# Score tiles of both heads in one double bank, and partition maxima by way of memory, in a fused attention and feed-forward kernel

## The chip, the cores and the metric

The kernel runs on one core of one Trainium2 chip. The metric is the device time of one execution in microseconds. The kernel before took 1224.53 us (median of three runs, 1223.8 to 1225.92). TensorE is called PE here (its weight loads PEld), VectorE DVE, ScalarE ACT, GpSimd POOL, and SyncE, which issues every DMA of this kernel, SP.

## The reference

Attention with a decay for 8 batches of 8 heads, 576 positions and 64 channels, and then a feed-forward layer with a quadratic gate over the 4608 tokens:

```python
log_f = np.log(np.clip(f, 0.0001, 1.0))
cum = np.cumsum(log_f, axis=-1)
scores = scale * q @ k.T + (cum[:, :, :, None] - cum[:, :, None, :])   # causal, scale = 1/8
attn = softmax(scores); attn_out = attn @ v
h = attn_out.reshape(4608, 512) @ w_in                                  # 512 -> 2048
g = np.where(h >= 1, h, np.where(h <= -1, 0.0, (h + 1) ** 2 / 4))
out = g @ w_out                                                         # 2048 -> 512
```

## The kernel before

The kernel works in f16 pairs: a number is scaled by a power of two and split into a high and a low f16 part, and a product takes three matmuls. The scale needs the largest magnitude of a tensor over all 128 partitions, which is what `across` (L112) gives: it takes one or two columns of maxima per partition, transposes them on PE (L120), reduces and clamps the row on DVE (L122, L123), spreads it over a diagonal (L127), broadcasts that to all partitions by a matmul with ones (L130) and copies the result (L131). It is called 48 times: for the 16 weight blocks (`weight_split`), for v of each of the 8 batches (`value_scale`), and for q and k together of 24 jobs (`measure`).

A job is a pair of heads of one batch. Batch 0 is cut into two row ranges, so there are 36 jobs. In the first 12, scores are made from f32 operands (`early_prepare`), and in the first 5 the probabilities are turned by PE (`turn_rows`); in that time the 16 weight blocks are loaded and split too. The other 24 jobs use split f16 operands and turn probabilities by DMA transposes (`pT`).

`scores` makes one block of 128 query rows: for each term and each of the two heads one matmul over 64 partitions, head 0 on partitions 0 to 63 and head 1 on 64 to 127 (L470). The outputs lie in tiles of the ring `s`, one bank for each head and two banks in all. The last block has 64 rows and 576 columns; both heads lie in the partitions of one tile of two banks, `big`, of which there is one. `big` also takes the values (`values`, `early_values`), the transposes of `early_prepare` and those of the decay sums. `weights` reads the scores on DVE (L559, with the decay row that POOL prepared from `ck` at L476 and L480), takes the exponential on ACT (L563), and splits the scaled probabilities into `pr` (L577 on ACT, L583 on DVE).

The feed-forward layer is cut into 144 units of 256 tokens and 256 hidden channels: `moe_front` (L645) into the ring `ph` of two banks, `moe_back` (L673) into `po0` and `po1`. Units are put between the rows of later jobs as tokens become ready; those left over run alone at the end.

v is loaded a second time for its maximum, by four loads per batch at L245 and reductions at L246. From batch 1 on these loads use the ring `ck` of three buffers, which also holds the decay rows that `load_decay` brings (L343).

The code gives the order in which work is recorded. The order on each engine and queue is made at build time by a scheduler with a model of the chip: it takes an instruction when its inputs, and a free buffer, are there by its model. Each engine then runs its list in order, and SP issues DMAs in order, each with its waits.

Of the kernel before, what the change touches and what calls it, by code (L numbers as in the profile page):

```python
# [8 lines left out]
F32 = mybir.dt.float32  # L9
# [37 lines left out]
def kernel(  # L47
# [41 lines left out]
    tiny = ctx.enter_context(tc.tile_pool(name="tiny", bufs=4))  # L89
    dram = ctx.enter_context(tc.tile_pool(name="dram", bufs=1, space=bass.MemoryType.DRAM))  # L90
    ps = ctx.enter_context(tc.tile_pool(name="ps", bufs=2, space=bass.MemoryType.PSUM))
    ps1 = ctx.enter_context(tc.tile_pool(name="ps1", bufs=1, space=bass.MemoryType.PSUM))
# [19 lines left out]
    def across(dst, m):  # L112

        n = m.shape[1]
        pt = ps.tile([P, 512], F32, name="s")
        nc.tensor.transpose(pt[0:n, 0:P], m, ident)  # L120
        top = tiny.tile([P, 1], F32, name="top", bufs=2)
        nc.vector.tensor_reduce(out=top[0:n], in_=pt[0:n, 0:P], axis=AX.X, op=ALU.max)  # L122
        nc.vector.tensor_scalar(  # L123
            out=top[0:n], in0=top[0:n], scalar1=LOW, scalar2=HIGH, op0=ALU.max, op1=ALU.min
        )
        dg = tiny.tile([P, 2], F32, name="dg", bufs=2)
        nc.vector.tensor_scalar(  # L127
            out=dg[0:n, 0:n], in0=ident[0:n, 0:n], scalar1=top[0:n], scalar2=None, op0=ALU.mult
        )
        nc.tensor.matmul(pt[:, P:P + n], lhsT=ones[0:n], rhs=dg[0:n, 0:n], start=True, stop=True)  # L130
        nc.vector.tensor_copy(dst, pt[:, P:P + n])  # L131


    ident = const.tile([P, P], F32, name="ident")
    make_identity(nc, ident)
    ones = const.tile([2, P], F32, name="ones")
    nc.gpsimd.memset(ones, 1.0)
    cum_d = dram.tile([B * H, S], F32, name="cum_d")
    cq = const.tile([P, NT5, B * H], F32, name="cq")

    def decay_sums():
# [93 lines left out]
    bsc = {}  # L235

    def value_scale(b):
        m4 = tiny.tile([P, NPAIR], F32, name="m4", bufs=2)
        for i in range(NPAIR):
            if b:  # L240
                st = two.tile([P, S], F32, name="ck", bufs=3)
            else:
                st = stage[:, i * S:(i + 1) * S]
            part = v[b, 2 * i:2 * i + 2].rearrange("h s d -> (h s d)").rearrange("(p n) -> p n", p=P)
            nc.sync.dma_start(st, part)  # L245
            nc.vector.tensor_reduce(  # L246
                out=m4[:, i:i + 1], in_=st, axis=AX.X, op=ALU.max, apply_absolute_value=True
            )
        m1 = tiny.tile([P, 1], F32, name="m1", bufs=2)
        nc.vector.tensor_reduce(out=m1, in_=m4, axis=AX.X, op=ALU.max)  # L250
        m = mv[:, b:b + 1]
        across(m, m1)
        if b:
            nc.vector.tensor_tensor(out=m, in0=m, in1=mv[:, b - 1:b], op=ALU.max)
        scale_of(sv[:, b:b + 1], pv[:, b:b + 1], m)
# [100 lines left out]
    def early_prepare(w):  # L356

        if w.p == 0:
            nc.vector.tensor_scalar(out=cq8, in0=cq[:, :, 0:2 * H], scalar1=8.0, scalar2=None, op0=ALU.mult)
        t_ = early_qk[(w.p + NQK) % 2]  # L360
        w.nsig, w.nalpha = -8.0, -0.125
        bh = w.b * H + 2 * w.hp
        w.cqs = cq8[:, :, bh:bh + 2]
        w.terms = ((t_[:, 0], t_[:, 1]),)
        for j in range(2):
            pt = ps1.tile([P, 1024], F32, name="big")
            t0 = 0 if j else w.r0
            n = w.s1 - P * t0
            for c0 in range(0, n, P):
                m = min(P, n - c0)  # L370
                nc.tensor.transpose(pt[:, c0:c0 + m], w.x32[j][0:m, c0:c0 + P], ident[0:m, 0:m])
            nc.scalar.activation(t_[:, j, 0:n], pt[:, 0:n], AF.Copy)
# [75 lines left out]
    def scores(w, r):  # L448
# [4 lines left out]
        for h in range(2):  # L453
            at.append((0, P) if r < LAST else (64 * h, 64 * h + 64))
            if r < LAST or h == 0:
                if r < LAST:
                    ring = sdr + more if w.p < NPE else sdr
                    sp = ps.tile([P, 512], F32, name="s")
                else:
                    ring = sd4 + [prs[LAST]] if w.p < NPE else sd4  # L460
                    sp = ps1.tile([P, 1024], F32, name="big")
                sd = ring[turn[r < LAST] % len(ring)]
# [56 lines left out]
    def early_values(w, x):  # L519
        if w.r0 == 0 and len(w.cuts) == 1:  # L520
            av = [ps1.tile([P, DM], F32, name="po0")]
        else:
            big = ps1.tile([P, 1024], F32, name="big")
            av = [big[:, 0:512], big[:, 512:1024]]
# [71 lines left out]
    def values(w, x):  # L596
        av = ps1.tile([P, 1024], F32, name="big")
        at = 512 - w.cuts[0][1] if len(w.cuts) == 2 else -w.s0
# [142 lines left out]
    load_decay(pairs[0], 1)  # L741
    prepare(pairs[0])
    value_scale(0)
    split_values(pairs[0])
    for p in range(njobs + 1):
# [3 lines left out]
        if w:  # L749
# [9 lines left out]
            def step(r):  # L759
                if r + 1 < w.r1:  # L760
                    scores(w, r + 1)
                if r == w.r1 - 2 and nxt:
                    load_decay(nxt, 1)
                    if nxt.hp == 0 and nxt.r0 == 0:
                        value_scale(nxt.b)
                    split_values(nxt)
                weights(w, r)
                if r == w.r1 - 1 and p + 2 < njobs:
                    measure(pairs[p + 2])
# [62 lines left out]
```

## Time and profile before

| | |
|---|---|
| median of three runs | 1224.53 us |
| profiled execution, its own time | 1223.2 us |
| its span, first to last instruction | 1221.4 us |
| mean granted TensorE clock | 0.954 |
| DMA moved | 152.21 MB in 408541 packets |

In the profile, a row of a group gives line, engine, operation, tiles, count, then busy time and mean length, then the idle time before these instructions and what ended it. The timeline gives start, length, engine, line, tiles and count. In the waits, a row names who waited, for whom, how long in total, how often, and the longest. PE's ends are modelled and matmuls overlap, so the steps between starts tell what a matmul costs PE's stream.

### The profile page before, as it was taken

Reading aid. Unit: us, or ns where it says so; the run is one execution under the profiler, and the core shown is the slowest. Engines: PE = TensorE matmul, PEld = TensorE weight load, DVE = VectorE, ACT = ScalarE, POOL = GpSimd, SP = SyncE. Lnnn points to the kernel's source line nnn. Section 1 sums busy time; section 2 is a strip of 40 time slices with the busy share of each in tenths; the row PEclk is TensorE's granted clock in tenths of the full one; section 3 lists DMA queues with packets and bytes.
Section 4 is the critical chain, followed back from the end, with each engine's and each line's share of the span. In section 5 each row is a group of like instructions: output and inputs, shape, how many; then the busy total and the mean of one; then the engine's idle time right before and its main releaser. Section 6 shows DMA issues by size and latency. Waiting matters only on the chain.

```text
span 1221.4 us, 24896 instructions
## 1 busy us (share of the span) xinstructions
PE 1118.6 (92%) x8865; PEld 683.2 (56%) x8865; DVE 854.6 (70%) x2423; ACT 762.5 (62%) x1558; POOL 443.9 (36%) x695
## 2 busy tenths in 40 slices
PE   5587677996799999999999999989999999999998
PEld 3354334553456565565655665655665566567665
DVE  6889888776877787777666767777877796522222
ACT  3574665774756676757666667666767687644443
POOL 4758644542633254334333224432443263100000
PEclk9878788899699999999999999999999999999999
DMA  8957543768866768657636736666966685300000
GB/s 230 278 149 199 135 123 79 138 126 175 172 129 140 146 131 162 126 120 141 126 88 134 150 69 126 140 138 123 172 123 135 143 154 114 72 24 2 18 19 18
DMA packets 408541, 152.21 MB, mean 125 GB/s; under 512 B 384225, under 2 KB 385249, under 8 KB 408417
## 3 DMA queue, kind: packets, MB, share of 16 engines
q1 hardware_dynamic: 408416, 150.63, 57.7%
q8 instruction: 69, 1.13, 0.4%
q14 instruction: 56, 0.45, 0.1%
HBM read 75.64 MB, written 9.58 MB: 70 GB/s over the span
## 4 chain that ended last, share of the span: by engine, by line
PE 38%; DVE 5%; DMA 3%; issue 2%; SPq 2%; ACT 2%; POOL 0%; DVEq 0%; ACTq 0%
PE ph L645 16%; PE po L673 16%; PE s L470 3%; PE big L603 2%; DMA ck<-in_v_dram 1%; DVE pr L583 1%; DVE sdr L559 1%; SPq L332 1%; DMA qk<-in_k_dram 1%; PE big L470 1%; DMA qk<-in_q_dram 1%; DVE u L656 1%; DVE g L659 1%; SPq L429 0%; ACT pr L577 0%
## 5 line engine op out<-in xcount | busy, mean ns | idle before, releaser
L645 PE MATMUL ph<-x,place 128*128 128x256 f16 (+3 forms) x4608 | 449.9, 250 | 12.6 <-DVE u L656 7.9
L673 PE MATMUL po<-place,g 128*128 128x512 f16 x1728 | 423.7, 384 | 9.4 <-DVE g L659 5.8
L645 PEld LDWEIGHTS <-place 128*128 128x128 f16 x4608 | 356.0, 99 | 115.2 <-issue 44.8
L673 PEld LDWEIGHTS <-g 128*128 128x128 f16 x1728 | 161.3, 99 | 184.8 <-issue 21.1
L476 POOL TENSOR_SCALAR sdr<-ck,nsig,cqs 128x128 f32<-128x128 f32 (+1 forms) x192 | 155.9, 815 | 229.8 <-DVE pr L583 218.1
L563 ACT ACTIVATE sdr<-sdr,nm 128x384 f32<-128x384 f32 (+1 forms) x248 | 138.5, 559 | 95.1 <-DVE nm L559 84.8
L470 PE MATMUL s<-qkT 64*128 64x384 f16 (+6 forms) x704 | 158.9, 359 | 23.3 <-DVE nm L559 21.6
L656 DVE SCALAR_TENSOR_TENSOR u<-ph,z,u 128x512 f32<-128x512 f32 x136 | 101.6, 747 | 108.8 <-ACT u L655 108.2
L654 ACT ACTIVATE u<-ph,z 128x512 f32<-128x512 f32 x136 | 104.7, 769 | 111.3 <-PE ph L645 110.6
L658 ACT ACTIVATE g<-u,z 128x512 f16<-128x512 f32 x136 | 97.7, 718 | 90.8 <-DVE u L656 90.2
L577 ACT ACTIVATE pr<-sdr,rc 128x384 f16<-128x384 f32 (+1 forms) x236 | 120.0, 556 | 38.7 <-DVE rc L574 16.9
L583 DVE SCALAR_TENSOR_TENSOR pr<-sdr,rc,pr 128x384 f16<-128x384 f32 (+2 forms) x232 | 126.3, 573 | 25.4 <-ACT pr L577 24.2
L476 POOL TENSOR_SCALAR sd<-ck,nsig,cqs 64x576 f32<-64x576 f32 x48 | 54.2, 1130 | 242.6 <-ACT qs L403 91.0
L659 DVE SCALAR_TENSOR_TENSOR g<-u,z,g 128x512 f16<-128x512 f32 x136 | 103.6, 761 | 38.4 <-ACT g L658 38.2
L559 DVE CUSTOM_DVE_ANT_0 sdr<-s,sdr,nalpha 128x128 f32<-128x128 f32 (+1 forms) x192 | 103.2, 545 | 23.1 <-PE s L470 17.0
L470 PEld LDWEIGHTS <-qkT 64*128 64x128 f16 (+1 forms) x864 | 47.9, 99 | 88.0 <-issue 66.5
L480 POOL TENSOR_SCALAR_AFFINE_SELECT sdr<-sdr 128x128 f32<-128x128 f32 x248 | 92.2, 381 | 10.9
L655 ACT ACTIVATE u<-u 128x512 f32<-128x512 f32 x144 | 89.8, 623 | 2.5
L603 PE MATMUL big<-pT,vs 128*64 128x320 f16 (+3 forms) x1098 | 72.8, 284 | 0.9 <-DVE nm L559 0.5
L381 DVE TENSOR_REDUCE m2q<-qk 128x1 f32<-128x640 f32 x48 | 39.2, 817 | 44.2 <-DMA qk<-in_q_dram 34.6
L603 PEld LDWEIGHTS <-vs 128*64 128x64 f16 x1098 | 49.9, 112 | 28.8 <-issue 10.1
L476 POOL TENSOR_SCALAR sdr<-ck,cq 128x384 f32<-128x384 f32 (+3 forms) x56 | 41.1, 734 | 62.5 <-DVE pr L583 34.1
(161 smaller groups left out, 1092.7 us busy)
## 6 DMA issues: line engine op xcount, KB each, us to landing
ck<-cum_d SPq DMA_DIRECT2D x64, 288.0 KB, 3.6
out_dram<-ot SPq DMA_DIRECT2D x36, 256.0 KB, 2.6
qk<-in_k_dram SPq DMA_DIRECT2D x64, 128.0 KB, 2.9
ck<-in_v_dram SPq DMA_DIRECT2D x28, 288.0 KB, 2.9
v<-in_v_dram SPq DMA_DIRECT2D x62, 128.0 KB, 2.8
qk<-in_q_dram SPq DMA_DIRECT2D x56, 128.0 KB, 2.7
place<-in_moe_w_in_dram SPq DMA_DIRECT2D x12, 512.0 KB, 5.4
place<-in_moe_w_out_dram SPq DMA_DIRECT2D x10, 512.0 KB, 6.7
```

What stands on the lines that cost most here:

```text
L470: nc.tensor.matmul(sds[h % len(sds)][1][p0:p1, c0:c1], lhsT=a[rows, q0 - w.s0:q0 - w.s0 + p1 - p0], rhs=b[rows, c0:c1], start=(i == 0), st ...
L476: nc.gpsimd.tensor_scalar(out=sd[p0:p1, 0:wid], in0=w.ck[h][p0:p1, 0:wid], scalar1=w.nsig if w.p < NQK else w.nsig[p0:p1], scalar2=w.cqs[p ...
L559: nc.vector.tensor_tensor_reduce(out=a, in0=sp[:, 0:wid], in1=a, scale=w.nalpha, scalar=BIG, op0=ALU.add, op1=ALU.min, accum_out=nm[:, i:i ...
L563: nc.scalar.activation(a, a, AF.Exp, bias=nm[:, i:i + 1], scale=-1.0, accum_out=sm[:, i:i + 1])
L577: nc.scalar.activation(pr[:, :, 0, i, :], a, AF.Copy, scale=rc[:, i:i + 1])
L583: nc.vector.scalar_tensor_tensor(out=pr[:, :, 1, i, :], in0=a, scalar=rc[:, i:i + 1], in1=pr[:, :, 0, i, :], op0=ALU.mult, op1=ALU.subtract,)
L603: nc.tensor.matmul(av[64 * h:64 * h + 64, at + s0:at + s1], lhsT=w.vs[:, vl, h, t, :], rhs=w.pT[:, t, pl, h, s0:s1], start=(t == 0 and pi ...
L645: nc.tensor.matmul(ph[:, fi, a0:a1], lhsT=wi[fb][:, wl, t, fi * P:(fi + 1) * P], rhs=xs[b][:, t, xl, s0:s0 + a1 - a0], start=(fi == 0 and ...
L654: nc.scalar.activation(u, h, AF.Relu, scale=z.u[:, i:i + 1], bias=z.h[:, i:i + 1])
L656: nc.vector.scalar_tensor_tensor(out=u, in0=h, scalar=z.t[:, i:i + 1], in1=u, op0=ALU.max, op1=ALU.min)
L659: nc.vector.scalar_tensor_tensor(out=g[:, 1], in0=u, scalar=z.r[:, i:i + 1], in1=g[:, 0], op0=ALU.mult, op1=ALU.subtract)
L673: nc.tensor.matmul(po[ch][i], lhsT=g[:, gl, fi * TC + i * P:fi * TC + (i + 1) * P], rhs=wo[fb][:, wl, fi, :], start=(first and fi == 0 and ...
```

## The change

It has three parts. The two heads' scores of a row block share one tile of two banks, one bank for each head; the ring `s` has two such tiles, and everything that used `big` now uses it, so PSUM has the same eight banks in use. `across` writes the columns of maxima to a row in memory, loads this row into all partitions, and reduces it on DVE; PE has no part in it. And v's loads for its maximum have a ring of their own, `vst`, and are recorded in the row blocks of the third pair of the batch before, with the maximum itself in the first row block of the fourth pair.

```diff
+    dram2 = ctx.enter_context(tc.tile_pool(name="dram2", bufs=4, space=bass.MemoryType.DRAM))
...
     def across(dst, m):
         n = m.shape[1]
-        pt = ps.tile([P, 512], F32, name="s")
-        nc.tensor.transpose(pt[0:n, 0:P], m, ident)
-        top = tiny.tile([P, 1], F32, name="top", bufs=2)
-        nc.vector.tensor_reduce(out=top[0:n], in_=pt[0:n, 0:P], axis=AX.X, op=ALU.max)
-        nc.vector.tensor_scalar(
-            out=top[0:n], in0=top[0:n], scalar1=LOW, scalar2=HIGH, op0=ALU.max, op1=ALU.min
-        )
-        dg = tiny.tile([P, 2], F32, name="dg", bufs=2)
-        nc.vector.tensor_scalar(
-            out=dg[0:n, 0:n], in0=ident[0:n, 0:n], scalar1=top[0:n], scalar2=None, op0=ALU.mult
-        )
-        nc.tensor.matmul(pt[:, P:P + n], lhsT=ones[0:n], rhs=dg[0:n, 0:n], start=True, stop=True)
-        nc.vector.tensor_copy(dst, pt[:, P:P + n])
+        d = dram2.tile([1, P * n], F32, name=f"row{n}")
+        nc.sync.dma_start(d.rearrange("o (p n) -> (o p) n", n=n), m)
+        rows = two.tile([P, 2 * P], F32, name="rows")[:, 0:n * P]
+        nc.sync.dma_start(rows, d.broadcast_to([P, n * P]))
+        nc.vector.tensor_reduce(
+            out=dst, in_=rows.rearrange("a (p n) -> a n p", n=n), axis=AX.X, op=ALU.max
+        )
+        nc.vector.tensor_scalar(out=dst, in0=dst, scalar1=LOW, scalar2=HIGH, op0=ALU.max, op1=ALU.min)
...
+    def value_part(b, i):
+        if b not in vmax:
+            vmax[b] = tiny.tile([P, NPAIR], F32, name="m4", bufs=2)
+        if b:
+            st = two.tile([P, S], F32, name="vst")
+        else:
+            st = stage[:, i * S:(i + 1) * S]
...
     def value_scale(b):
-        m4 = tiny.tile([P, NPAIR], F32, name="m4", bufs=2)
-        for i in range(NPAIR):
-            if b:
-                st = two.tile([P, S], F32, name="ck", bufs=3)
...
-            pt = ps1.tile([P, 1024], F32, name="big")
+            pt = ps.tile([P, 1024], F32, name="s")
...
                     ring = sdr + more if w.p < NPE else sdr
-                    sp = ps.tile([P, 512], F32, name="s")
                 else:
                     ring = sd4 + [prs[LAST]] if w.p < NPE else sd4
-                    sp = ps1.tile([P, 1024], F32, name="big")
+                if h == 0:
+                    pair = ps.tile([P, 1024], F32, name="s")
+                sp = pair[:, 512 * h:512 * h + 512] if r < LAST else pair
...
     def values(w, x):
-        av = ps1.tile([P, 1024], F32, name="big")
+        av = ps.tile([P, 1024], F32, name="s")
...
                 if r == w.r1 - 2 and nxt:
                     load_decay(nxt, 1)
-                    if nxt.hp == 0 and nxt.r0 == 0:
-                        value_scale(nxt.b)
                     split_values(nxt)
                 weights(w, r)
+                if w.r1 == NT5 and w.b + 1 < B:
+                    i = r - w.r0
+                    if w.hp == NPAIR - 2:
+                        for part in range(i, i + 1 if r < LAST else max(i, NPAIR)):
+                            if part < NPAIR:
+                                value_part(w.b + 1, part)
+                    if w.hp == NPAIR - 1 and i == 0:
+                        value_scale(w.b + 1)
```

The order on PE in the fourteenth job (its operands are `qkT_3210` before and `qkT_3115` after), at the third row block, 384 columns wide; `s_3597` is head 0 and `s_3598` head 1. Before:

```order
L470 LDWEIGHTS qkT_3210
L470 MATMUL s_3597<-qkT_3210 128x384
L645 LDWEIGHTS place0_90
L645 MATMUL ph_3646<-x_80,place0_90 128x192
...
L645 MATMUL ph_3646<-x_80,place0_90 128x192
L470 LDWEIGHTS qkT_3210
L470 MATMUL s_3598<-qkT_3210 128x384
```

The same row block after, where both heads lie in `s_3493` and L466 and L641 are the lines of scores and feed-forward:

```order
L466 MATMUL s_3493<-qkT_3115 128x384
L466 LDWEIGHTS qkT_3115
L466 MATMUL s_3493<-qkT_3115 128x384
L641 LDWEIGHTS place0_90
L641 MATMUL ph_3541<-x_81,place0_90 128x64
```

Before, 19 feed-forward matmuls stood between the three matmuls of one head and the three of the other. After, the six stand in one run, the heads taking turns.

On DVE, a maximum of q and k (tile `m2q_7190`, reduced at L376) and its return from memory (L120), in a job of the second half. After:

```order
L376 TENSOR_REDUCE m2q_7190<-qk32_0_114 128x1
L579 SCALAR_TENSOR_TENSOR pr1_5960<-sdr_2_119,rc_5967,pr1_5960 128x2x128
L579 SCALAR_TENSOR_TENSOR pr1_5960<-sdr_3_120,rc_5967,pr1_5960 128x2x128
L567 TENSOR_SCALAR rc_6068<-sm2_6063 128x2
L570 RECIPROCAL rc_6068<-rc_6068 128x2
L652 SCALAR_TENSOR_TENSOR u_6027<-ph_5978,z_5435,u_6027 128x512
L579 SCALAR_TENSOR_TENSOR pr2_6061<-sdr_0_117,rc_6068,pr2_6061 128x3x128
L579 SCALAR_TENSOR_TENSOR pr2_6061<-sdr_1_118,rc_6068,pr2_6061 128x3x128
L120 TENSOR_REDUCE mk_7193<-rows_7196 128x2
L555 ISA sdr_2_119,nm_6177<-s_6046,sdr_2_119,nalpha_5296 128x512
```

Seven instructions stand between the reduction and the one that reads the row; the score minimum behind it (L555, which was L559) waits with it. On SP the same maximum stands between this job's k loads and the decay rows, `qkT` of the next job and `pT` of the current one:

```order
L327 DMA qk32_0_114<-in_k_dram 128x4x64 x2
L331 DMA qk32_0_114<-in_k_dram 64x2x64
L117 DMA row2_7194<-m2q_7190 128x2
L119 DMA rows_7196<-row2_7194 128x256
L338 DMA ck_6168<-cum_d_88 128x576
L338 DMA ck_6409<-cum_d_88 128x576
L405 DMA_TRANSPOSE qkT_6416<-qs_6411 128x20x128
L585 DMA_TRANSPOSE pT_5925<-pr0_5926 128x4x128
```

Before, SP went from the k loads to the decay rows with no store and no load of a row between them.

More of the change, by code (lines that the diff above doesn't have):

```diff
@@ L118, in across @@
         n = m.shape[1]
-        pt = ps.tile([P, 512], F32, name="s")
-        nc.tensor.transpose(pt[0:n, 0:P], m, ident)
-        top = tiny.tile([P, 1], F32, name="top", bufs=2)
-        nc.vector.tensor_reduce(out=top[0:n], in_=pt[0:n, 0:P], axis=AX.X, op=ALU.max)
-        nc.vector.tensor_scalar(
-            out=top[0:n], in0=top[0:n], scalar1=LOW, scalar2=HIGH, op0=ALU.max, op1=ALU.min
-        )
-        dg = tiny.tile([P, 2], F32, name="dg", bufs=2)
-        nc.vector.tensor_scalar(
-            out=dg[0:n, 0:n], in0=ident[0:n, 0:n], scalar1=top[0:n], scalar2=None, op0=ALU.mult
-        )
-        nc.tensor.matmul(pt[:, P:P + n], lhsT=ones[0:n], rhs=dg[0:n, 0:n], start=True, stop=True)
-        nc.vector.tensor_copy(dst, pt[:, P:P + n])
+        d = dram2.tile([1, P * n], F32, name=f"row{n}")
[4 more added lines that the diff above has]
+            out=dst, in_=rows.rearrange("a (p n) -> a n p", n=n), axis=AX.X, op=ALU.max
+        )
+        nc.vector.tensor_scalar(out=dst, in0=dst, scalar1=LOW, scalar2=HIGH, op0=ALU.max, op1=ALU.min)
     ident = const.tile([P, P], F32, name="ident")
     make_identity(nc, ident)
-    ones = const.tile([2, P], F32, name="ones")
-    nc.gpsimd.memset(ones, 1.0)
     cum_d = dram.tile([B * H, S], F32, name="cum_d")
@@ L235 @@
     bsc = {}
-    def value_scale(b):
-        m4 = tiny.tile([P, NPAIR], F32, name="m4", bufs=2)
-        for i in range(NPAIR):
-            if b:
-                st = two.tile([P, S], F32, name="ck", bufs=3)
[L242 to L247, printed above, removed]
-            )
+    vmax = {}
+    def value_part(b, i):
[5 more added lines that the diff above has]
+            st = stage[:, i * S:(i + 1) * S]
+        part = v[b, 2 * i:2 * i + 2].rearrange("h s d -> (h s d)").rearrange("(p n) -> p n", p=P)
+        nc.sync.dma_start(st, part)
+        nc.vector.tensor_reduce(
+            out=vmax[b][:, i:i + 1], in_=st, axis=AX.X, op=ALU.max, apply_absolute_value=True
+        )
+    def value_scale(b):
         m1 = tiny.tile([P, 1], F32, name="m1", bufs=2)
-        nc.vector.tensor_reduce(out=m1, in_=m4, axis=AX.X, op=ALU.max)
+        nc.vector.tensor_reduce(out=m1, in_=vmax[b], axis=AX.X, op=ALU.max)
         m = mv[:, b:b + 1]
@@ L365, in early_prepare @@
         for j in range(2):
-            pt = ps1.tile([P, 1024], F32, name="big")
+            pt = ps.tile([P, 1024], F32, name="s")
             t0 = 0 if j else w.r0
@@ L522, in early_values @@
         else:
-            big = ps1.tile([P, 1024], F32, name="big")
+            big = ps.tile([P, 1024], F32, name="s")
             av = [big[:, 0:512], big[:, 512:1024]]
@@ L742 @@
     prepare(pairs[0])
+    for i in range(NPAIR):
+        value_part(0, i)
     value_scale(0)
```

## The prediction

> **What bounds the kernel now.** I read the page's busy times first, then the windows of three stages, then the waits and the groups by line inside the middle stage. On the page:
>
> ```profile
> span 1221.4 us, 24896 instructions
> PE 1118.6 (92%) x8865; PEld 683.2 (56%) x8865; DVE 854.6 (70%) x2423; ACT 762.5 (62%) x1558; POOL 443.9 (36%) x695
> ```
>
> The windows of the first twelve jobs (scores in f32, weights converted), of the other 24 (scores in f16), and of the tail with feed-forward units alone:
>
> ```profile
> core 0: us, PE busy (x) PEld busy (x) DVE busy (x) ACT busy (x) POOL busy (x), PEclk, DMA share, GB/s
> 0.00:286.00 286.00, 221.66 (x1247) 125.35 (x1248) 228.31 (x704) 173.63 (x391) 154.96 (x223) 0.86 0.66 164
> 286.00:1052.00 766.00, 731.76 (x6261) 445.16 (x6258) 576.51 (x1651) 517.07 (x1064) 288.93 (x472) 0.98 0.66 133
> 1052.00:1222.00 170.00, 165.13 (x1364) 112.65 (x1360) 49.76 (x70) 71.80 (x104) 0.00 (x0) 1.00 0.10 23
> ```
>
> The middle stage holds 63% of the span. PE is busy 732 of its 766 us (96%), DVE 75%, ACT 68%: there the time is PE's stream, and PE idles 34 us. In the first stage no engine is full; in the tail PE is, with work that the change leaves alone. So the change is worth what it takes out of PE's stream between 286 and 1052 us, less what the other queues then cannot follow.
>
> **Scores.** PE's timeline (start, length, engine, line, tiles, count):
>
> ```profile
> 617.30 0.66 PE L470 MATMUL s<-qkT 64*128 64x384 f16 x3
> 617.89 0.40 PE L645 MATMUL ph<-x,place 128*128 128x64 f16 x4
> ...
> 622.04 0.82 PE L470 MATMUL s<-qkT 64*128 64x512 f16 x3
> 622.79 0.83 PE L645 MATMUL ph<-x,place 128*128 128x256 f16 x6
> 623.55 0.82 PE L470 MATMUL s<-qkT 64*128 64x512 f16 x3
> 624.31 0.28 PE L645 MATMUL ph<-x,place 128*128 128x256 f16 x1
> ```
>
> ```profile
> 428.43 0.67 PE L470 MATMUL s<-qkT 64*128 64x384 f16 x6
> 429.03 1.04 PE L673 MATMUL po<-place,g 128*128 128x512 f16 x4
> ```
>
> ```profile
> 626.48 1.69 PE L645 MATMUL ph<-x,place 128*128 128x256 f16 x14
> ```
>
> Starts count, since ends are modelled. The run of 14 gives (1.69 - 0.27) / 13 = 0.109 us for 256 columns, 0.42 ns a column. Three matmuls of 512 columns should then take 0.65 us, but the next line starts 0.75 us later; six of 256 should take 0.65 and take 0.76. So every step between a matmul on half the rows and one on all rows costs 0.105 us, and **a visit to the scores costs 0.21 us** beside its columns. And six 384-column matmuls, three of each head, took 0.60 us (428.43 to 429.03), as long as three of one head alone (617.30 to 617.89): heads on partitions 0-63 and 64-127 run side by side, **the second head is free**, if nothing stands between them.
>
> Counted over PE's order, the f16 scores of 128-row blocks are 576 matmuls and 184,320 columns in both kernels. Before, they stand in 161 visits, 24 of which hold both heads, with 18,688 columns beside the other head; after, in 100 visits, 97 with both heads, with 89,856. Before: 161 x 0.21 + 165,632 x 0.42 ns = 103 us. After: 100 x 0.21 + 94,464 x 0.42 ns = 61 us. **Minus 42 us.** The last block (64 rows) already ran its heads side by side.
>
> **Maxima off PE.** A maximum in the middle stage:
>
> ```profile
> 604.12 0.27 PE L120 MATMUL s<-ident,m2q 128*2 128x128 f32 x1
> 604.23 2.73 PE L645 MATMUL ph<-x,place 128*128 128x192 f16 x46
> 606.89 0.38 PE L130 MATMUL s<-dg,ones 2*128 2x2 f32 x2
> 607.20 0.29 PE L645 MATMUL ph<-x,place 128*128 128x192 f16 x2
> ```
>
> The transpose holds the stream 0.11 us, the broadcast 0.31 and a step of 0.1 ahead of it: 0.52 us. The groups inside the window 286 to 1052:
>
> ```profile
> L130 PE MATMUL s<-dg,ones 2*128 2x2 f32 (+1 forms) x58 | 10.4, 258 | 3.0 <-DVE dg L127 2.9
> ...
> L120 PE MATMUL s<-ident,m 128*1 128x128 f32 x6 | 1.6, 272 | 1.9 <-DVE m L250 1.9
> ```
>
> 58 broadcasts are 29 maxima, with two lost or outside records some 31: **minus 16 us**, the 5 us of waits in these rows not counted. PE's order of values and last blocks has some 20 more changes of tile shape after than before: **plus 2 us**.
>
> DVE gives up four small instructions for two:
>
> ```profile
> L122 DVE TENSOR_REDUCE top<-s 1x1 f32<-1x128 f32 (+1 forms) x48 | 12.6, 272 | 4.2 <-PE s L120 4.0
> ...
> L246 DVE TENSOR_REDUCE m<-ck 128x1 f32<-128x576 f32 x28 | 21.0, 752 | 26.2 <-DMA ck<-in_v_dram 26.0
> ```
>
> The new reduction reads 128 or 256 numbers per partition: between 0.27 and 0.75 us by these rows, I take 0.4, since 256 lies nearer to 128. With the clamp it replaces one of the same kind, so DVE loses some 0.2 us each; nothing waits for that.
>
> **The trip through memory.** No row shows it. The nearest are the store of the sums and the loads of 128 KB:
>
> ```profile
> cum_d<-x SPq DMA_DIRECT2D x1, 144.0 KB, 2.3
> ...
> qk<-in_k_dram SPq DMA_DIRECT2D x42, 128.0 KB, 2.7
> place<-in_moe_w_out_dram SPq DMA_DIRECT2D x10, 512.0 KB, 6.7
> ```
>
> The trip lies between 2 x 2.3 and 2 x 6.7 us; I take 2.3 + 2.7 = 5.0, since 128 KB is the size of the load for two columns. The way over PE was no shorter where queues were full: for the first weight block DVE's rows stand 16 us apart.
>
> ```profile
> 27.19 0.14 DVE L216 TENSOR_REDUCE m<-ms 128x1 f32<-128x2 f32 x1
> ...
> 43.41 0.16 DVE L131 COPY mi<-s 128x1 f32<-128x1 f32 x1 [1.10 <-PE s L130]
> ```
>
> What counts is how much stands on DVE between the maximum and its return. The groups give the durations:
>
> ```profile
> L583 DVE SCALAR_TENSOR_TENSOR pr<-sdr,rc,pr 128x384 f16<-128x384 f32 (+2 forms) x232 | 126.3, 573 | 25.4 <-ACT pr L577 24.2
> ...
> L656 DVE SCALAR_TENSOR_TENSOR u<-ph,z,u 128x512 f32<-128x512 f32 x136 | 101.6, 747 | 108.8 <-ACT u L655 108.2
> ...
> L381 DVE TENSOR_REDUCE m2q<-qk 128x1 f32<-128x640 f32 x48 | 39.2, 817 | 44.2 <-DMA qk<-in_q_dram 34.6
> ```
>
> In the piece of the order shown with the change, four L583, one L656 and two small ones stand between: 4 x 0.57 + 0.75 + 0.35 = 3.4 us. Added up so over the whole order, 18 of the 24 maxima of q and k have about 3.5 us; those of the weights have 3 to 31, mostly over 5. Where it is 3.5, DVE stands 5.0 - 3.5 = 1.5 us at least, and those behind it are a score minimum, on which the next scores wait. 18 x 1.5 = 27 us of DVE; PE has a feed-forward unit in hand that covers part. Bounds: nothing, and 24 x 5.0 = 120 us. I take **plus 20 us**, near the 27.
>
> The Trainium skill ("DMA: Bandwidth & Descriptors", Anatomy of one DMA) gives a fixed cost of about 2.0 us per DMA, most of it the receipt of the write, and calls HBM the heaviest target, which speaks against two small DMAs in a row. By it alone the trip would be 4.0 us and the term about 9; the 2.3 us of this trace's store agree, its loads are slower.
>
> **Waits that go.** In the middle stage and, below, in the first:
>
> ```profile
> PE s L470 <- DVE nm L559: 13.3, 8, 6.1
> ...
> POOL sd L476 <- DMA ck<-cum_d: 73.4, 22, 13.3
> ```
>
> ```profile
> PE s L120 <- DVE m L216: 14.8, 3, 10.4
> ...
> PE s L130 <- DVE dg L127: 11.4, 6, 3.0
> ```
>
> Values and the last block now share the ring of two double banks, so a row's scores can still wait for DVE: I leave the 13.3 us where they are. Own buffers for v free the decay rows' ring; POOL's 73.4 us are off the path, so I count nothing. In the first stage PE's 26 us behind maxima go, but there DVE and ACT set the pace, and the order puts the weights' ends later among the jobs; f32 heads side by side help a little. I take **minus 4 us**, bounds minus 25 and plus 20.
>
> **Sum.** -42 - 16 + 2 + 20 - 4 = -40 us. Against the profiled execution's own 1223.2 us that is 1183; the median of the runs is 1224.5, 1.3 above, so **1184 us**.
>
> **The rivals.** *SP becomes the bound (slower).* One job's issues in SP's timeline:
>
> ```profile
> 640.69 6.82 SPq L589 DMA_TRANSPOSE pT<-pr  x4
> 647.60 2.71 SPq L592 DMA_TRANSPOSE pT<-pr  x2
> ...
> 655.05 3.63 SPq L410 DMA_TRANSPOSE qkT<-qs  x1
> ```
>
> These 13.2 us and a dozen loads of about 0.5 are 19 us of a job's 766 / 24 = 31.9. The new store stands right behind the k loads, so SP holds for k's landing (2.7), the reduction (0.8) and the store's landing (2.3): 5.8 us, with two issues 6.7. SP then has 25.7 us in a job; behind the hold stand the decay loads, the next qkT and this job's pT, for which POOL and PE wait. If its other waits come to more than 6.2 us a job, the jobs run at SP's pace and slower than now; at 7.2 us it is +24 us, **1248**. For it: one queue, in order, held 24 times. Against it: of 31.9 us it issues only 19 now, so it stands 13 us in a job with PE full, and much of the hold may fall into those.
>
> *The clock gives it back.* Two windows:
>
> ```profile
> 300.00:350.00 50.00, 40.45 (x355) 24.39 (x355) 42.85 (x146) 35.95 (x79) 27.15 (x42) 0.76 0.80 160
> ...
> 500.00:550.00 50.00, 50.00 (x389) 30.71 (x387) 34.81 (x109) 30.53 (x58) 13.89 (x22) 1.00 0.70 142
> ```
>
> Where PE idled 10 of 50 us the granted clock was 0.76. If PE falls to some 92% busy and the clock to 0.96, 3% of 670 us come back, and the time is about **1204**. The Trainium skill ("TensorE: Matmul & The Clock Gate", HAM oscillation) warns of idle gaps over about 3.4 us, after which the array restarts at half clock; the low clock of 300 to 350 agrees, and by that rule shorter gaps would cost nothing.
>
> *No change.* DVE or ACT set the jobs' pace and PE only idles more: **1224**. Against it: 500 to 550, PE 50 of 50 and DVE 35. *The heads don't run side by side in one tile*: only the visits, 13 us, and the maxima are left, about **1213** after the trip's cost; the run of six speaks against it.
>
> **Chances.** Forecast (1152 to 1200) 0.58; clock 0.12; no pairing 0.03; no change 0.04; SP 0.15; better than 1152, where the waits go too, 0.08. A measurement tells 0.2% (2.4 us). Faster 0.80, same 0.05, slower 0.15. From 1152 to 1232 the range leaves out the 0.08 and two thirds of SP's 0.15.
>
> **What would show it.** Runs of six in PE's timeline with the next line 0.60 us behind at 384 columns; PE busy in the stage near 680 us; no L120 and L130 on PE; DVE waiting for rows from memory about 1 to 2 us each, under 50 us in all; SP's wait for the row's landing about 2.3 us. I am wrong if DVE or PE wait for these rows, or for decay rows and pT behind them, over 60 us in all, or if the first stage ends far from 282 us.

## The result, and the profile after

The changed kernel takes **1392.68 us** (median of four runs, 1386.13 to 1397.27; the profiled one took 1397.27, its span is 1395.5), the kernel before 1224.66 in the same runs: a ratio of 1.137, interval 1.131 to 1.142. The forecast was 1184, faster; it is 168 us slower, and outside the range.

The first lines of its page, and its windows, cut at the first and the last f16 score as before (286 and 1052 us there, 391 and 1226 here):

```profile
span 1395.5 us, 24501 instructions
PE 1080.0 (77%) x8721; PEld 666.2 (48%) x8721; DVE 835.6 (60%) x2327; ACT 764.4 (55%) x1558; POOL 421.6 (30%) x694
```

```profile
core 0: us, PE busy (x) PEld busy (x) DVE busy (x) ACT busy (x) POOL busy (x), PEclk, DMA share, GB/s
0.00:391.00 391.00, 203.74 (x1133) 118.17 (x1133) 232.73 (x714) 173.42 (x387) 140.97 (x218) 0.74 0.72 138
391.00:1226.00 835.00, 711.02 (x6240) 435.32 (x6232) 551.56 (x1542) 517.18 (x1064) 280.61 (x476) 0.93 0.64 119
1226.00:1395.50 169.50, 165.20 (x1364) 112.67 (x1360) 51.32 (x72) 73.79 (x108) 0.00 (x0) 1.00 0.09 23
```

The first stage is 105 us longer, the middle 69, the tail the same. The engines do not do more: PE is busy 39 us less and DVE 19 us less than before, ACT 2 us more. In the middle PE idled 34 us; now it idles 124. So the time went into waits, and these rows of the waits of the whole span (who waited for whom, us in total, times, longest) say which are new:

```profile
DVE mk L120 <- DMA rows<-row: 94.7, 24, 7.2
...
PE s L466 <- DVE nm L555: 56.3, 14, 9.6
...
DVE m L120 <- DMA rows<-row: 37.6, 8, 7.6
...
DVE mi L120 <- DMA rows<-row: 32.1, 4, 8.8
...
DVE mv L120 <- DMA rows<-row: 12.2, 5, 8.9
DVE m L206 <- DMA row<-m: 11.9, 3, 7.0
```

DVE stands 177 us for rows from memory, in 41 of 48 maxima, and 19 us more (the last row, and 7.3 us at L245) until a store has read a buffer that it wants to write again. PE is behind it: at its scores it waits 56 us for score minima (22 before). One q/k maximum in DVE's timeline and in SP's (start, length, engine, line, tiles, count, the idle time ahead in brackets):

```profile
1067.95 0.82 DVE L376 TENSOR_REDUCE m2q<-qk 128x1 f32<-128x640 f32 x1 [0.33 <-DMA qk<-in_k_dram]
1068.69 0.87 DVE L579 SCALAR_TENSOR_TENSOR pr<-sdr,rc,pr 128x256 f16<-128x256 f32 x2
1069.48 0.16 DVE L567 TENSOR_SCALAR rc<-sm 128x2 f32<-128x2 f32 x1
1069.67 0.17 DVE L570 RECIPROCAL rc<-rc 128x2 f32<-128x2 f32 x1
1069.91 0.75 DVE L652 SCALAR_TENSOR_TENSOR u<-ph,z,u 128x512 f32<-128x512 f32 x1
1070.58 1.34 DVE L579 SCALAR_TENSOR_TENSOR pr<-sdr,rc,pr 128x384 f16<-128x384 f32 x2
1076.90 0.42 DVE L120 TENSOR_REDUCE mk<-rows 128x2 f32<-128x256 f32 x1 [4.98 <-DMA rows<-row]
1077.23 0.74 DVE L555 CUSTOM_DVE_ANT_0 sdr<-s,sdr,nalpha 128x512 f32<-128x512 f32 x1
```

```profile
1068.80 0.35 SPq L117 DMA_DIRECT2D row<-m2q  x1
1072.53 0.34 SPq L119 DMA_DIRECT2D rows<-row  x1
```

From the store's issue to the reduction are 8.1 us; on DVE stand 3.2 us of work in between, and then it stands 4.98. Right behind it wait the score minima (L555), and PE behind these: its last block ends at 1073.56 (1072.63 + 0.93, a modelled end), and it stood 5.15 us until 1078.71.

```profile
1072.63 0.93 PE L466 MATMUL s<-qkT 64*64 64x512 f16 x12
1078.71 0.74 PE L599 MATMUL s<-pT,vs 128*64 128x64 f16 x4 [5.15 <-DVE nm L555]
```

The landings (KB each, median us) of most of the weights' loads, and of the trip's two halves, for one column of maxima (weights and v; 0.5 and 64 KB) and for two (q and k; 1.0 and 128 KB):

```profile
place<-in_moe_w_in_dram SPq DMA_DIRECT2D x12, 512.0 KB, 5.7
place<-in_moe_w_out_dram SPq DMA_DIRECT2D x10, 512.0 KB, 7.6
...
rows<-row SPq DMA_DIRECT2D x24, 128.0 KB, 4.4
...
rows<-row SPq DMA_DIRECT2D x24, 64.0 KB, 4.9
...
row<-m SPq DMA_DIRECT2D x24, 0.5 KB, 8.9
row<-m2q SPq DMA_DIRECT2D x24, 1.0 KB, 3.6
```

So the trip takes 3.6 + 4.4 = 8.0 us for q and k, and 8.9 + 4.9 = 13.8 for weights and v, most of which run in the first stage. And SP is held there, as its waits between 0 and 391 us show; behind each hold stand weights, decay rows and transposes:

```profile
SPq L119 <- DMA row<-m: 91.9, 14, 11.1
```

### The profile page after: what moved, and what is told of

Its sections match the earlier page's. It is cut to its first block, busy times and chain, and to the rows that moved or that the text cites. A ratio compares the mean times of both kernels' runs of the same rounds, so it can differ in the third digit from the quotient of the medians.

```text
span 1395.5 us, 24501 instructions
## 1 busy us (share of the span) xinstructions
PE 1080.0 (77%) x8721; PEld 666.2 (48%) x8721; DVE 835.6 (60%) x2327; ACT 764.4 (55%) x1558; POOL 421.6 (30%) x694
## 5 line engine op out<-in xcount | busy, mean ns | idle before, releaser
L669 PE MATMUL po<-place,g 128*128 128x512 f16 x1728 | 439.9, 400 | 97.0 <-ACT g L654 58.8
L641 PE MATMUL ph<-x,place 128*128 128x256 f16 (+3 forms) x4608 | 436.7, 252 | 39.8 <-DVE u L652 15.5
L641 PEld LDWEIGHTS <-place 128*128 128x128 f16 x4608 | 361.2, 100 | 123.2 <-issue 59.2
L472 POOL TENSOR_SCALAR sdr<-ck,nsig,cqs 128x128 f32<-128x128 f32 (+1 forms) x192 | 149.4, 781 | 413.9 <-DVE pr L579 297.0
L559 ACT ACTIVATE sdr<-sdr,nm 128x384 f32<-128x384 f32 (+1 forms) x248 | 138.0, 557 | 145.0 <-DVE nm L555 139.8
L466 PE MATMUL s<-qkT 64*64 64x512 f16 (+11 forms) x1056 | 134.9, 365 | 75.5 <-DVE nm L555 56.3
L599 PE MATMUL s<-pT,vs 128*64 128x64 f16 (+3 forms) x1098 | 85.6, 305 | 68.8 <-DVE nm L555 34.9
L555 DVE CUSTOM_DVE_ANT_0 sdr<-s,sdr,nalpha 128x128 f32<-128x128 f32 (+1 forms) x192 | 99.3, 545 | 31.0 <-PE s L466 23.2
L599 PEld LDWEIGHTS <-vs 128*64 128x64 f16 x1098 | 58.1, 120 | 94.8 <-issue 55.2
L476 POOL TENSOR_SCALAR_AFFINE_SELECT sdr<-sdr 128x128 f32<-128x128 f32 x248 | 87.6, 364 | 9.7
L376 DVE TENSOR_REDUCE m2q<-qk 128x1 f32<-128x640 f32 x48 | 39.2, 817 | 65.8 <-DMA qk<-in_q_dram 34.7
L466 PEld LDWEIGHTS <-qkT 64*128 64x128 f16 (+1 forms) x864 | 33.7, 101 | 72.5 <-issue 58.4
```

The lines of the kernel that those rows point to most:

```text
L466: nc.tensor.matmul(sds[h % len(sds)][1][p0:p1, c0:c1], lhsT=a[rows, q0 - w.s0:q0 - w.s0 + p1 - p0], rhs=b[rows, c0:c1], start=(i == 0), st ...
L472: nc.gpsimd.tensor_scalar(out=sd[p0:p1, 0:wid], in0=w.ck[h][p0:p1, 0:wid], scalar1=w.nsig if w.p < NQK else w.nsig[p0:p1], scalar2=w.cqs[p ...
L555: nc.vector.tensor_tensor_reduce(out=a, in0=sp[:, 0:wid], in1=a, scale=w.nalpha, scalar=BIG, op0=ALU.add, op1=ALU.min, accum_out=nm[:, i:i ...
L559: nc.scalar.activation(a, a, AF.Exp, bias=nm[:, i:i + 1], scale=-1.0, accum_out=sm[:, i:i + 1])
L599: nc.tensor.matmul(av[64 * h:64 * h + 64, at + s0:at + s1], lhsT=w.vs[:, vl, h, t, :], rhs=w.pT[:, t, pl, h, s0:s1], start=(t == 0 and pi ...
L641: nc.tensor.matmul(ph[:, fi, a0:a1], lhsT=wi[fb][:, wl, t, fi * P:(fi + 1) * P], rhs=xs[b][:, t, xl, s0:s0 + a1 - a0], start=(fi == 0 and ...
```

## The experiments

Eighteen kernels. The stages end at the first and the last f16 score of the one profiled execution of each kernel; the tail is 169 to 170 us in each. The last two columns are the sums of all rows "DVE ... <- DMA ..." in the waits of each stage: how long DVE stood for any transfer (rows, stores, q, k, v, weights).

| kernel | time, us | first stage | middle | DVE for DMAs, first | middle |
|---|---|---|---|---|---|
| before | 1224.7 | 286 | 766 | 22 | 59 |
| e12 v in first stage as before | 1201.7 | 300 | 732 | 19 | 49 |
| e11 early PSUM as before | 1206.4 | 304 | 732 | 26 | 48 |
| e8 the same, fixed tiles (scores overwritten) | 1208.2 | 299 | 738 | 26 | 48 |
| e16 e11 without v loads | 1212.4 | 300 | 742 | 27 | 67 |
| e1 pairs, v loads | 1220.3 | 321 | 728 | 34 | 49 |
| e4 v loads | 1224.3 | 299 | 752 | 26 | 56 |
| e3 pairs | 1231.1 | 314 | 742 | 37 | 71 |
| e18 before, stores alone | 1264.0 | 310 | 780 | 50 | 73 |
| e14 e1, stores alone | 1281.0 | 388 | 722 | 101 | 50 |
| e6 reduction later | 1303.1 | 383 | 756 | 126 | 77 |
| e13 only q/k by memory | 1313.3 | 320 | 821 | 40 | 145 |
| e5 e1, trips unread | 1319.7 | 403 | 740 | 116 | 62 |
| e10 e5, loads free | 1327.7 | 412 | 742 | 114 | 56 |
| e17 before, trips unread | 1328.2 | 338 | 818 | 74 | 122 |
| e15 e5, more buffers | 1340.7 | 432 | 739 | 143 | 60 |
| e7 POOL's queue | 1351.8 | 390 | 793 | 114 | 121 |
| e19 without v loads | 1354.3 | 351 | 838 | 97 | 146 |
| e2 memory alone | 1362.3 | 352 | 835 | 105 | 150 |
| after | 1392.7 | 391 | 835 | 139 | 158 |

### The change in its parts

e2 is the kernel before with the new `across` alone; e3 with the pair tiles alone (`across` takes its tile from the pairs' ring); e4 with the v loads alone; e1 is the changed kernel with the old `across`:

```diff
-        d = dram2.tile([1, P * n], F32, name=f"row{n}")
...
+        pt = ps.tile([P, 1024], F32, name="s")
+        nc.tensor.transpose(pt[0:n, 0:P], m, ident)
...
```

> The changed kernel with the partition maxima back on PE (their tile is taken from the ring of score pairs); the pairs and the v loads stay changed. Theory A (the way through memory is what costs: in the changed kernel DVE stands 188 us for rows from memory, and PE starves behind it): the loss goes, DVE's waits for rows with it, and the pairs show their gain of 103 - (105 visits x 0.21 us + 95,872 columns x 0.42 ns = 62) = 41 us: 1184 us, 1165 to 1215. Rival B (one ring of two double banks for scores, values and last blocks couples PE to DVE's row blocks; PE waits 107 us for the score minima in the changed kernel): the loss stays, 1340 to 1400. Rival C (the v loads in own buffers crowd SP and the DMA queues): the loss stays here too, 1340 to 1400.

> The kernel before with one part of the change alone: the partition maxima by way of memory. Score rings, the double bank and the v loads are those of before. Theory A (the way through memory costs): the whole loss of the change, without the gain of the pairs: 1392.7 + 41, less what wider spacing of PE hides, 1370 to 1450, with DVE waiting for rows 150 to 220 us in all. Rival B (the merged ring): 1200 to 1235, PE's 16 us for the maxima less. Rival C (v loads): the same, 1200 to 1235.

> The kernel before with one part of the change alone: both heads' scores in one tile of two banks, in a ring of two that also takes values, last blocks and, here, the maxima's transposes. Theory A: 103 - (97 visits x 0.21 us + 94,208 columns x 0.42 ns = 60) = 43 us less on PE: 1181 us, 1165 to 1215. Rival B (the merged ring couples PE to DVE): 1300 to 1400, PE waiting for score minima 60 us or more. Rival C (v loads): 1165 to 1215.

> The kernel before with one part of the change alone: v's loads for its maximum in buffers of their own, recorded in the third pair of the batch before. Theory A and rival B: PE's work is the same, so 1215 to 1235; POOL's wait for decay rows under the 73 us of before. Rival C (these loads crowd SP and the DMA queues): 1260 or more, with decay rows and transposes landing later.

Ratios: e1 0.996 (0.994 to 0.999), e2 1.114 (1.110 to 1.118), e3 1.006 (1.003 to 1.009), e4 1.001 (0.999 to 1.003). The way through memory carries the loss (e2, 8 us below theory A's range); rivals B and C fall as its cause. But the pairs miss their 1184 too: their gain is in the middle (766 to 728 in e1), and the first stage gives 35 of it back (286 to 321). The middle of e1:

```profile
320.50:1049.00 728.50, 679.63 (x6223) 430.37 (x6225) 559.12 (x1590) 505.34 (x1052) 288.44 (x470) 0.98 0.65 130
```

PE is busy 52 us less than the 732 of before, at the same clock. After the change it was busy 711, at 0.93: 711 x 0.93 = 661 and 680 x 0.98 = 666 are nearly the same work. By this estimate the lower clock took some 30 us, and more if the maxima, which e1's PE still makes, are taken off the 666. After the stand of 5.15 us above the granted clock is low, and 1.00 again from 1085 to 1090 (columns as in the windows above):

```profile
1068.00:1074.00 6.00, 5.56 (x72) 3.81 (x71) 3.81 (x8) 3.61 (x9) 3.53 (x6) 1.00 0.06 2
1074.00:1079.00 5.00, 0.29 (x4) 0.23 (x3) 2.10 (x6) 0.98 (x3) 1.08 (x2) 0.67 1.07 211
1079.00:1082.00 3.00, 2.66 (x8) 0.84 (x7) 2.90 (x13) 2.69 (x6) 1.07 (x3) 0.50 0.46 104
```

The Trainium skill ("TensorE: Matmul & The Clock Gate", HAM oscillation) warns of idle gaps over about 3.4 us; the gap of 5.15 us above and the lower clock agree.

### DVE's stand or SP's hold?

e5 is e1 with the stores and loads put in again behind each maximum, unread:

```diff
         nc.vector.tensor_copy(dst, pt[:, P:P + n])
+        d = dram2.tile([1, P * n], F32, name=f"row{n}")
+        nc.sync.dma_start(d.rearrange("o (p n) -> (o p) n", n=n), m)
+        rows = two.tile([P, 2 * P], F32, name="rows")[:, 0:n * P]
+        nc.sync.dma_start(rows, d.broadcast_to([P, n * P]))
```

e6 is the changed kernel with the sending recorded earlier and the reduction tied behind a later row block's minimum (`lastnm` holds them):

```diff
+            nc.vector.tensor_copy(dst[:, 0:1], lastnm[-1][:, 0:1])
         nc.vector.tensor_reduce(
             out=dst, in_=rows.rearrange("a (p n) -> a n p", n=n), axis=AX.X, op=ALU.max
         )
```

e7 is the changed kernel with the row's two DMAs issued by POOL:

```diff
-        nc.sync.dma_start(rows, d.broadcast_to([P, n * P]))
+        nc.gpsimd.dma_start(rows, d.broadcast_to([P, n * P]))
```

> The kernel of e1 (pairs, v loads, maxima on PE) with the stores and loads of the rows put in again, all 48 of each, and nobody reading the rows. SP is held for each store's landing as in the changed kernel, and the DMA engines carry the same bytes; DVE has nothing to wait for. Theory A (what costs is DVE standing in its in-order stream for the rows): 1215 to 1250 us, near e1's 1220. Rival D (what costs is SP, held behind each store while decay rows, transposes and loads queue up: 155 us of such waits in the changed kernel): 1330 to 1400, as the changed kernel, with PE and POOL waiting for DMAs.

> The changed kernel with the same trips through memory, but with DVE's reduction of the rows put later: q and k are measured three row blocks before a job's end and the rows are reduced behind the last row block's minimum (tied to it by a copy of that minimum into the result's tile, 0.15 us), weights one row block later than before. In DVE's order 60 to 120 instructions now stand between a q/k maximum and its return, in place of 7 to 19; the weights' gaps grow less. Theory A: DVE's waits for rows fall from 177 us to under 60, and the time to 1200 to 1280. Rival D (SP's hold): the stores and loads and SP's hold are the same, 1330 to 1400.

> The changed kernel with the rows' stores and loads issued by POOL in place of SP, so SP is no longer held for them. Rival D (SP's hold): most of the loss goes, 1220 to 1290. Theory A: the trip is still 6 to 13 us long and DVE stands for it as long as before: 1340 to 1420, with DVE waiting for rows 130 us or more; POOL held for the landings adds to it.

Ratios 1.079 (1.075 to 1.084), 1.065 (1.061 to 1.070) and 1.102 (1.097 to 1.108): e5 and e6 fall between the two theories' ranges, e7 into A's. By stages they come apart. **In the middle of these kernels, DVE's stand decides.** With SP held as in the change (67.6 us in 19 waits for the stores of q and k, 57.7 in 20 there) and nobody reading, it takes 740 us in e5; with the reduction later, 756 in e6; 835 in the change. DVE's waits of e6 between 383 and 1139 us, those for DMAs, have no rows left:

```profile
DVE m2q L394 <- DMA qk<-in_q_dram: 60.0, 19, 7.3
...
DVE m2q L394 <- DMA qk<-in_k_dram: 17.0, 13, 3.5
```

The 158 us of stands fell by 81, the stage by 79. **In the first stage** e5 is as long as the change, with no row read: there theory A alone is wrong. Its waits between 0 and 403 us show what DVE stands for instead, loads that SP issued late:

```profile
DVE m L254 <- DMA vst<-in_v_dram: 40.7, 9, 10.1
DVE u L200 <- DMA place<-in_moe_w_in_dram: 30.3, 4, 11.3
DVE m L221 <- DMA row<-m: 11.9, 3, 6.0
```

And e7 is no cure: POOL is held in place of SP (78 and 61 us behind the two kinds of store), and its stores land no sooner:

```profile
row<-m POOLq DMA_DIRECT2D x24, 0.5 KB, 9.7
```

The Trainium skill ("DMA: Bandwidth & Descriptors", Issuing engines are not separate DMA queues) says that transfers of all issuing engines run on the same 16 DMA engines and interleave. The 9.7 us beside SP's 8.9 agree.

### The first stage

e10 is e5 with the rows loaded from a line of the decay sums, e13 the changed kernel with the old `across` for one column and the new one for two; e14 and e15 are e5 with 16 buffers in place of 2 for the weights' and v's maxima (and 8 in place of 4 for those of q and k), e14 without the rows' loads:

```diff
-        nc.sync.dma_start(rows, d.broadcast_to([P, n * P]))
+        nc.sync.dma_start(rows, cum_d[0:1, 0:n * P].broadcast_to([P, n * P]))
```

> The kernel of e5 (maxima on PE; rows stored and loaded with no reader) with one thing changed: each row's load reads a line of the decay sums instead of the row just stored, so it doesn't wait for the store's landing. The issues and bytes are the same. In e5 the first stage took 403 us against e1's 320, the middle 740 against 728. Theory D2 (SP held for the landing, 8.4 us at the median for the 0.5 KB stores, delays the weights' and v's loads behind it in the first stage): the first stage ends at 310 to 340, the time is 1220 to 1250. Rival G (the 96 more transfers load SP and the DMA engines): it stays near 400, 1295 to 1325.

> The changed kernel with the maxima of the weights and of v back on PE; those of q and k go through memory as in the change. So 24 of the 48 trips are left, all in the middle stage. Theory A with D2 (in the first stage SP's hold costs, in the middle DVE's stand): the first stage ends at 310 to 335 us as in e1, the middle lasts 810 to 840 as in the changed kernel, the time is 1300 to 1340. Rival: if the trips of the weights in the first stage shift everything behind them, the middle falls to 760 or less with them.

> The kernel of e5 (maxima on PE, rows stored and loaded with no reader; first stage 403 us against e1's 320) without the rows' loads, and with 16 buffers for the maxima in place of 2, so that neither SP nor DVE stands for a store's landing. SP still holds at each store until DVE has made the maximum. Theory D2 (the hold for the landing costs): the first stage ends at 312 to 340 us, the time is 1212 to 1242. Rival J (the store, waiting in SP's order for DVE's maximum, is enough): 360 us or more, and 1265 or more.

> The kernel of e5 with all stores and loads of the rows, and 16 buffers for the maxima in place of 2, so DVE no longer waits for a store to have read a maximum before it makes the next but one (26 us in e10's first stage, 12 us in the changed kernel). SP's hold for the landing stays. Theory D2 (SP's hold costs): the first stage stays at 380 to 410 us, the time at 1290 to 1330. Rival K (DVE's stand for these buffers costs): 345 us or less, and 1265 or less.

e13 (1.074, 1.071 to 1.077) hit: with the trips of weights and v gone, the first stage is back at 320, and the q/k trips alone make the middle 821 us, 93 more than e1's. (The expectation put all 24 there; 3 of their rows are read in the first stage, 21 in the middle.) e10 (1.086) came out close to rival G's numbers, but it separates little: its loads, free of the stores, all went into the first stage, where SP stood 56 us for their own buffers. e14 (1.045) fell into rival J's ranges, with a first stage of 388 us and no store's landing waited for; e15 (1.095) lay above both of its theories. So no single cause holds, but in all these kernels the v loads stand in the way. Reductions of v in the first stage, in the windows of this tile: 5 of 28 before, 24 in e1, 20 after (the expectation of e19, below, puts them higher). The last:

```profile
core 0: us, DVE busy (x), PEclk, DMA share, GB/s
0.00:391.00 391.00, 14.74 (x20) 0.74 0.72 138
391.00:1226.00 835.00, 5.99 (x8) 0.93 0.64 119
```

With buffers of their own these loads wait for nothing but one another's two buffers, and the scheduler draws them forward into the stage in which the weights come in. So the last three put the trips on the kernel before (e17: e5's lines and 16 buffers; e18: e17 without the loads), and took the v loads out of the change (e19: `value_scale` as before, in the ring `ck`):

```diff
-        m1 = tiny.tile([P, 1], F32, name="m1", bufs=2)
+        m1 = tiny.tile([P, 1], F32, name="m1", bufs=16)
```

> The kernel before, its maxima on PE as they were, with all 48 stores and loads of the rows added and nobody reading them, and 16 buffers for the maxima so that DVE doesn't stand for a store. Score rings and v loads are those of before. In e2 (rows read by DVE, else as before) the first stage took 352 us against 286, and the middle 835 against 766. Theory A2 (DVE's stand for the rows is the cause in both stages): the first stage ends at 282 to 305 us, the time is 1220 to 1250. Theory D2 (SP's hold for the landing is the cause in the first stage): 330 to 360 us, and 1270 to 1310.

> As e17 without the rows' loads: 48 stores that nobody waits for. Theories A2 and D2: first stage 282 to 305 us, time 1218 to 1240. Rival J (a store that waits in SP's order for DVE's maximum is enough): the first stage 325 us or more, 1265 or more.

> The changed kernel with the v loads as before the change (ring of the decay rows, old place); pairs and trips through memory stay. In the kernels with the changed v loads most of these 288 KB loads stand in the first stage (in the changed kernel and in e1, nearly all of the 28; before, 8), and in e14 DVE stood 60 us for them there with no row to wait for. Theory L (the v loads, pulled forward, are part of the first stage's 391 us): it ends at 340 to 368 us, the time is 1345 to 1378. Rival: they fill gaps only, 380 us or more, and 1385 to 1405.

e17 (1.087, 1.083 to 1.092) decides against theory A2: the first stage goes to 338 with no row read, as D2 said; its middle, 818, and its time neither had foreseen. SP's first row below is the hold between 0 and 338.5 us; the others are DVE's stands between 338.5 and 1156.5, for q (32 us before) and v (19):

```profile
SPq L136 <- DMA row<-m: 51.0, 8, 9.0
```

```profile
DVE m2q L386 <- DMA qk<-in_q_dram: 84.1, 20, 8.7
DVE m L251 <- DMA ck<-in_v_dram: 28.0, 16, 4.1
```

e18 (1.033, 1.030 to 1.036) lies between: 48 stores that nobody waits for cost 24 us of the first stage and 14 of the middle. On the rings of before, then, the trip's cost mounts in steps: stores alone (e18) plus 24 and 14 us, with loads behind the landing (e17) plus 52 and 52, with DVE reading the rows (e2) plus 66 and 69. Here most of it comes without a row being read, in the middle too, where e5 on the pairs' rings lost 12 us. Rings and v loads differ between e17 and e5 at once, so why the middle bears the hold in one and not in the other stays open. e19 (1.106, 1.102 to 1.109) hit: without the v loads the changed kernel's first stage is 351 us, not 391. So of the 105 us there 65 belong to the trips (e2 has the same 352) and 40 to v loads drawn forward beside them; in e4, without trips, these loads cost 12.

**What joins these.** In the kernels with pairs the middle follows DVE's stands for DMAs: 728 + (stands - 49), from e1, gives 837 after (835), 824 in e13 (821), 756 in e6 (756), 741 in e5 (740), 800 in e7 (793), 825 in e19 (838). On the rings of before, 766 + (stands - 59) gives 780 in e18 (780), 829 in e17 (818), 857 in e2 (835). Whether DVE stands for a row, or for a q/k load that a held SP issued late, it costs about its length, with misses of up to 22 us. In the first stage both rise together, but by this law several miss by 10 to 35 us. e6 and e13 changed the stands on purpose; for the others it is a relation that the traces show.

### A version that beats both

e8 and e11 keep e1, with PSUM in the first twelve jobs as before the change. e8 does so with fixed tiles, and there a row block's scores are overwritten by the next block's before they are read, so its time is no evidence by itself; e11 with a pool that is closed at the 13th job. e12 takes the second batch's v loads back to the ring `ck`; e16 is e11 with all v loads as before:

```diff
+        if p == NQK:
+            early_banks.close()
+            banks[:] = [ctx.enter_context(tc.tile_pool(name="psm", bufs=2, space=bass.MemoryType.PSUM)), False]
```

> The kernel of e1 (pairs, v loads, maxima on PE) with PSUM used in the first twelve jobs as before the change: two single banks for f32 scores and maxima, one double bank for values, transposes and last blocks; from the 13th job on two double banks as in e1. Theory E (the pairs gain 38 us in the middle stage of e1, 728 us against 766, and the merged ring gives 35 back in the first, 320 us against 286): the first stage ends at 280 to 298 us, the middle lasts 725 to 750, and the time is 1180 to 1210. Rival F (the first stage's loss in e1 comes of the v loads or of the order that the scheduler finds, not of the ring): it ends at 310 to 325 and the time stays at 1210 to 1228.

> The kernel of e1 (pairs, v loads, maxima on PE) with PSUM of the first twelve jobs as before the change (two single banks and one double bank, released as in the kernel before), and the ring of two double banks from the 13th job on. Theory E (the merged ring costs the first stage some 20 to 35 us): it ends at 284 to 302 us, the middle lasts 725 to 750, the time is 1183 to 1212. Rival F (the v loads or the order that the scheduler finds cost the first stage, not the ring): 310 to 325, and the time 1212 to 1228.

> The kernel of e11 with v's loads for the maximum of the second batch, which fall into the first stage, taken back to the ring of the decay rows and to their old place; those of later batches stay in own buffers. In e4 the v loads alone moved the end of the first stage from 286 to 298.5 us and shortened the middle from 766 to 752. Theory H (these loads, early, take DMA time and DVE from the weights): the first stage ends 5 to 14 us sooner than e11's, the time is 5 to 14 us lower, 1175 to 1203. Rival I (both are chance of the scheduler's order): the first stage within 4 us of e11's or longer, and the time within 5 us.

> The kernel before with the pairs alone, and these only from the 13th job on: PSUM of the first twelve jobs as before, maxima on PE, v loads as before. So e11 without the v loads. If the v loads cost the first stage its 298.5 us in e4 and 304 in e11, and gain 14 us in the middle: first stage 284 to 292, middle 738 to 756, time 1192 to 1218. If the first stage stays at 298 or more, the v loads are not its cause.

e8 0.986 (0.982 to 0.990), e11 0.986 (0.983 to 0.989), **e12 0.982 (0.980 to 0.985), 1201.7 us**, e16 0.991 (0.987 to 0.994): gains of under 2%, with intervals that stay below 1. The merged ring cost the first stage 17 us (e1 321, e11 304), 2 us beyond the end that theory E allowed. e12 against e11 (3.5 us in the first stage, 4.8 in the time) lies inside rival I's bounds and just short of theory H's 5, and within their intervals: H and I stay undecided. e16 has the pairs alone in the middle: 742, minus 24; with v's loads elsewhere 732. Why these first stages are 300 us and not 286 is open: e16, with the v loads as before, has it too, so by its own expectation they are not the cause.

## Why the prediction was wrong

Two terms of the sum failed, both about the trip through memory: plus 20 us for DVE behind the trip came to 93, and minus 4 us for the first stage came to plus 105. That is 73 and 109 us of the 209 between forecast and result.

- **"The trip ... I take plus 20 us" failed in its size.** It took 2.3 + 2.7 = 5.0 us from a 144 KB store and 128 KB loads; the trip takes 8.0 and 13.8, the second beyond the 2 x 6.7 that the text allowed. The work on DVE in between was right (3.5 forecast, 3.2 in the case shown), so in the middle DVE stands 90 / 21 = 4.3 us, not 1.5, and for 21 maxima, not 18:

```profile
DVE mk L120 <- DMA rows<-row: 89.7, 21, 7.2
```

PE's feed-forward unit in hand did not cover it: the trips of q and k cost the middle 93 us (e13 against e1), within the bounds of 0 to 120 that the text gave, at the far end from the value taken. The page of the Trainium skill cited there ("DMA: Bandwidth & Descriptors", Anatomy of one DMA: about 2.0 us fixed, for DMAs that GpSimd issues) would have given still less; for the 0.5 KB store, issued by SP, the measured 8.9 us decide.
- **"Minus 4 us" for the first stage** failed in kind, and is the larger miss: it came to plus 105, against bounds of -25 and +20. It counted what leaves PE and not what SP and DVE get: 21 of the 24 stores of weights and v, with SP held 92 us behind them, loads that come late after it, and 84 us in which DVE stands for rows. "Those of the weights have 3 to 31, mostly over 5" would have covered a trip of 5.0 us, not one of 13.8. That a wait stands in an in-order queue was argued for the 24 q/k maxima alone. Of the 105 us, 65 go with the trips (e2, e19) and 40 with the v loads beside them (e19); how the 65 divide between SP's hold and DVE's stand is shown on the rings of before only (52 of 66 us with no row read, e17 and e2).
- **"Own buffers for v ... I count nothing"** was wrong in two ways: 14 us less in the middle (e4; e1 against e3), 40 more in the first stage beside the trips (e19). A ring of their own let the scheduler move these loads far ahead.
- **Scores, "minus 42 us", was right for PE's stream** (52 us less busy in e1's middle; six 384-column matmuls with the next line 0.60 us behind). As time it is 24 alone (e16) and 38 with the v loads (e1): the rest became idle PE. The merged ring's price in the first stage (17 us) was not counted.
- **The maxima's "minus 16"** can't be seen in the time: the clock moved more. By busy time x clock, an estimate, e2's middle gives 742 x 0.94 = 697 against 732 x 0.98 = 717 before, which is near it; after the change 661 against e1's 666 is not.
- **The rivals.** "SP becomes the bound", with 0.15 and 1248, named the right queue and the right direction; on the pairs' ring trips that nobody reads, and behind which SP holds, add only 12 us to the middle and 82 to the first stage (e5 against e1); on the rings of before they add 52 to each (e17 against before). The clock's loss came, beside the stands and not in place of them; its 3% should have been 2% by the 0.98 and 0.96 that it goes from.
- **What would show it** did: of the 60 us of waits for rows that would prove it wrong there were 177, and the first stage ended at 391, not near 282. SP's wait for a row's landing, "about 2.3 us", was 2.9 in the middle (57.7 in 20) and 6.6 in the first stage (91.9 in 14).

## What to carry to other kernels

A trip through memory is priced by the landings of its own two transfers under the load of its own stage, and by what is queued behind each in-order waiter: the engine that reads and the queue that issues. Taking 0.5 us off the full engine is no gain if the second engine in line then stands 4 us, since the full one starves behind it. And a buffer ring that looks like a bottleneck can be what keeps loads out of a crowded stage; judge a change by stages, since e1's gain of 38 us and loss of 35 hide in a ratio of 0.996.

## What was not expected of the hardware

A store of 0.5 KB, one number from each of 128 partitions, landed in 8.9 us at the median. That is longer than the medians of three of the four groups of 512 KB loads in the same kernel (4.5, 5.7 and 7.6 for 28 loads; the other four took 13.7), and than that of the 1.0 KB stores, two numbers from each partition (3.6). The DMA engines' share was 0.72 in the first stage and 0.64 in the middle. The stage alone doesn't explain it: in the middle of e2, where both stores occur, they landed in

```profile
row<-m2q SPq DMA_DIRECT2D x22, 1.0 KB, 3.8
row<-m SPq DMA_DIRECT2D x6, 0.5 KB, 8.1
```

and the 18 of e2's first stage in 7.9. e18's stores, which nobody waits for, landed there in 8.0 (0.5 KB) and 4.5 (1.0 KB). So the smaller store was the slower one in the same stage. Whether that comes of its form or of the transfers just ahead of it is open: no run here has that store in an idle stage, or changes its form.
